# Landmark attention and MLP on one core: half the second layers by seven half-size products, W1 centred by GpSimd

## The chip, the cores and the metric

One Trainium2 chip, one core. The metric is the device time of one execution in microseconds (us), the median over several runs. A profiled execution, taken once, gives the trace from which the single durations come. Engines: PE (TensorE), DVE (VectorE), ACT (ScalarE), POOL (GpSimd), SP (SyncE, which here issues most transfers).

## The reference

q, k and v are (8 batches, 8 heads, 576 tokens, 64) in float32. Attention is approximated through 32 landmarks per head, each the mean of 18 neighbouring tokens; the MLP stands behind it with a residual.

```python
A  = sm(q, k_lm);  Bm = sm(q_lm, k_lm);  C = sm(q_lm, k)     # softmax(scale * a @ b^T)
Z  = Bm^T / (norm1(Bm) * norminf(Bm) + 1e-6)
for _ in range(6):
    Z = 2 * Z - Z @ Bm @ Z
x  = heads side by side of (A @ Z @ C @ v)                    # (8, 576, 512)
xn = (x - mean) / sqrt(var + 1e-6) * g_ln                     # over the 512 columns
out = x + relu(xn @ W1) @ W2                                  # W1 512 x 2048, W2 2048 x 512
```

## The kernel before

All matmul operands are float16, sums in PSUM and the stream x are float32. Every instruction goes through a small helper that keeps the program's order on its engine, so in the profile nearly all of DVE, ACT and POOL stand on line 69 and all matmuls on line 75; groups are told apart by tiles. The order of the work is therefore the order in which the Python code issues it.

**Attention.** Batches come as 0, 1, 2, then the pairs (3, 4) and (5, 6), then 7. `Coming` prepares the queries, keys and values of a batch or pair: SP loads into a staging buffer `stg`, POOL casts to float16 (`nat`, `natv`), DVE turns 32x32 blocks (`turn`, tile `xT`), landmark sums come from POOL (`asum`, `s`) or DVE (`part`), and a matmul spreads them (`spread`). `next_cast` and `next_job` each take one such piece; `prepare(c, casts, jobs)` takes several. `attention2` is a generator: scores against landmarks (tiles psb, psec, psea), the gram and its row and column sums, six iterations of Z on 32x32 tiles (tile `st`: DVE scales, PE multiplies, hand over hand), then `rows_of`, which writes x in 36 blocks of 128 tokens (`xblk`) through PE and ACT and takes their variance on DVE (`block_done`). The softmax quotient of A is a multiplication of `ea` by reciprocals (`normalize`, line 734): by POOL, in batch 1 by DVE.

**MLP.** LayerNorm is folded in. Its mean is taken out of W1: `less_mean(f)` computes the negative column mean of quarter f, and `center_w1` adds it to W1 (eight DVE instructions of 128x1024, in the first eight steps of batch 2's attention); batches 0 and 1 use W1 as it is with a correction. Its 1/deviation is multiplied in at the end (`rstds`, from ACT in `deviations`). The first layer never forms x: `product_of_heads(f)` multiplies the small Z side with a quarter of W1 (tile `m`), `chunk(m)` multiplies that by A, four matmuls of 288 columns, and ACT writes the relu into 128 of the 2,048 hidden columns (`hT`). The second layer takes, for each of the 4 or 5 row blocks of a batch, 16 matmuls of 128x512 into one PSUM bank; `finish_block` adds bank times rstd into x on DVE and `store` sends it out on SP's queue. Even batches have four blocks; the last 64 tokens go with the next odd batch (`keep_tail`, POOL), which has five.

**How they interleave.** `mlp()` is one stream of matmul columns: the second layer of batch b, and every 2,048 columns a piece of the first layer of batch b+1. `fill(n)` draws n x 512 columns from it between the steps of the attention generators; the list `steps` says how many, and how many casts and jobs of the next set are done in each. Behind the last attention the stream runs on by itself. Batch 0's first layer is written out by hand in the loop over m before that, with the first two row blocks of its second layer accumulated beside it and batch 1's scores behind its chunk 12.

PSUM: four single banks handed out by turns (`banks`; one of them goes to attention, so three remain; tile `bank` in the profile), and two tiles of two banks each (`ps2`: psh, psea, psec, psd, pscv, pszt, pszc).

Of the kernel before, what the change touches and what calls it, by code (L numbers as in the profile page):

```python
# [9 lines left out]
FP16 = mybir.dt.float16  # L10
# [3 lines left out]
ALU = mybir.AluOpType  # L14
AX = mybir.AxisListType

P = 128
# [3 lines left out]
def kernel(  # L21
# [13 lines left out]
    DM = H * D  # L35
# [5 lines left out]
    KCH = DM // P  # L41
    MCH = HID // P
# [11 lines left out]
        name=nc.get_next_instruction_name(), act_func_set_id=6, ins=[], outs=[]))  # L54
# [3 lines left out]
    stage = ctx.enter_context(tc.tile_pool(name="stage", bufs=6))  # L58
# [12 lines left out]
    dve, pool, scalar = Ordered(nc.vector), Ordered(nc.gpsimd), Ordered(nc.scalar)  # L71
    act = scalar.activation

    def MM(o, l, r, rb=0, cb=0, start=True, stop=True, skip=False):
        keep(nc.tensor.matmul(o, l, r, start=start, stop=stop, tile_position=(rb, cb),  # L75
                              skip_group_check=(skip or cb != 0)))
# [85 lines left out]
    for i in range(NV):  # L162
        t = const.tile([P, U, NJ, 2, D + 1], FP16, name=f"natv{i}")
# [18 lines left out]
    w1_16 = wpool.tile([P, KCH, HID], FP16, name="w1_16")  # L182
    w2_16 = wpool.tile([P, MCH, DM], FP16, name="w2_16")
# [6 lines left out]
    def less(f):  # L190
        return less_[f // 2][:, f % 2, :]
# [77 lines left out]
    banks = Banks()  # L269
# [6 lines left out]
    x_blk = {}  # L276
# [40 lines left out]
    def normalize(ea, engine):  # L317
        engine.tensor_tensor(out=ea, in0=ea, in1=divisors(ea), op=ALU.mult)
# [196 lines left out]
    class Coming:  # L515
# [25 lines left out]

        def next_job(self):
            if self.jobs:
                f, i = self.jobs.pop(0)
                f(i)

        def load(self, i, queue=nc.sync):
# [116 lines left out]
    def attention2(bs, c):  # L664
        units, lm, xT = c.units, c.lm, c.xT
        W = len(units)
# [21 lines left out]
        ea = []  # L688
# [31 lines left out]
        late, z0 = bs[0] == 1, 2 if bs[0] == 1 else 0  # L720
# [8 lines left out]
        for it in range(6):  # L729
            st = iterate(p1, st, it, W)  # L730
            if it < W // 2:
                ea += scores_q((2 * it, 2 * it + 1), lm, xT)
            if W // 2 <= it < W // 2 + W:
                normalize(ea[it - W // 2], dve if late else pool)
            if late and it == 4:
                product(0)
            if late and it == 5:
                product_done()
            yield it < W // 2
# [30 lines left out]
    stats_of, rstds = {}, {}  # L770
# [16 lines left out]
    def deviations(b):  # L787
        n = 4 + b % 2
        if b not in rstds and blocks_done.get(b) == n:
            lnv = mstat.tile([P, 5], FP32, name="lnv", tag="lnv")  # L790
            act(lnv[:, 0:n], stats_of[b][:, 0:n, 1], AF.Ln, bias=eps_ln[:], scale=UP * UP)
            rstds[b] = mstat.tile([P, 5], FP32, name="rstd", tag="rstd")
            act(rstds[b][:, 0:n], lnv[:, 0:n], AF.Exp, scale=-0.5)

    def store(j, x, cols, both=False):
        for i in range(2):
            b, c = divmod(2 * j + i, NJ)
            half = x[ds(64 * i, 64), cols]
# [17 lines left out]
        if c1 == KCH:  # L816
            scalar.copy(less(f), psf_of.pop(f)[:])

    def center_w1(f, c=0, n=KCH):
        o = w1_16[:, ds(c, n), ts(f, 512)]  # L820
        dve.tensor_tensor(out=o, in0=o, in1=less(f)[:, None, :].broadcast_to([P, n, 512]),
                          op=ALU.add)

    class First:
        def __init__(self, b):
# [12 lines left out]

        def product_of_heads(self, f):
            self.m16[f] = mprod.tile([P, U, 512], FP16, name="m16", tag="m16")  # L840
            psm = [banks.take([P, 512]) for _ in range(U)]
            for r in range(2):
                for e in range(2):
                    for u in range(U):
                        rows, cb = ds(64 * e, 64), 32 * (2 * (e ^ u) + r)
                        MM(psm[u][ds(cb, 32), :], self.zt[rows, r, self.w0 + u, :],
                           w1_16[rows, 2 * u + r, ts(f, 512)], rb=64 * e, cb=cb,
                           stop=self.sums is None, skip=True)
            for u in range(U):
                if self.sums is not None:  # L850
                    MM(psm[u], self.sums[:, u, :], less(f), start=False, skip=True)
                if u == 0 or f == 0:
                    scalar.copy(self.m16[f][:, u, :], psm[u])
                else:
                    dve.tensor_copy(out=self.m16[f][:, u, :], in_=psm[u])

        def chunk(self, m):
            psh = ps2.tile([P, 2, 512], FP32, name="psh", tag="p2")
# [21 lines left out]
    def keep_tail(b):  # L880
        if b % 2 == 0:
            room_for(b + 1)
            pool.tensor_copy(out=hTs[b + 1][:, :, 0:64], in_=hTs[b][:, :, S - 64:S])

    def finish_block(b, u, pso, part=None):
# [8 lines left out]
        if part != 0:  # L894
            x_blk.pop(j)

    def second_layer(b):
        hT = hTs[b]
        blocks = range(4 + b % 2) if b else (2, 3)
        for u in blocks:  # L900
            last = b == B - 1 and u == 4
            for part in ((0, 1) if last else (None,)):
                n = DM if part is None else DM // 2
                cols = ts(part or 0, n)
                pso, bank = banks.hold([P, n]), banks.last
                for m in range(MCH):
                    MM(pso[:], hT[:, m, ts(u, P)], w2_16[:, m, cols],
                       start=(m == 0), stop=(m == MCH - 1))
                    if m >= 8:
# [54 lines left out]
    sets = [Coming((1,), ("k0", "k1", "q0", "q1"))]  # L964
# [9 lines left out]
    def prepare(c, casts, jobs):  # L974
        for _ in range(casts):
            if c.casts and (c.parts[c.casts[0]][0] == "v" or len(c.n16) < 6):
                c.next_cast()
                load_ahead()
        for _ in range(jobs):
            c.next_job()  # L980

    warm(36, 160)
    a0 = attention0()
# [14 lines left out]
    b1 = sets[0]  # L998
# [31 lines left out]
    def blocks_0_and_1(m):  # L1030
        for u in range(2):
            MM(accs[u][:], hTs[0][:, m, ts(u, P)], w2_16[:, m, :],
               start=(m == 0), stop=(m == MCH - 1))

    a1 = attention2((1,), b1)
    for m in range(MCH):
        l1.chunk(m)
        if m == 0:
            scale_w1(7, 1, scalar)
        if m == 1:  # L1040
            l1.product_of_heads(1)
# [12 lines left out]
        if 2 <= m < 10 or m == 13:  # L1054
            b1.next_job()
        if m >= 10:
            blocks_0_and_1(2 * (m - 10))
            blocks_0_and_1(2 * (m - 10) + 1)
    keep_tail(0)
    for m in range(12, MCH):  # L1060
        blocks_0_and_1(m)
        if m == 12:
            assert not b1.jobs
            banks.order.remove(3)
            next(a1)
            deviations(0)
    for u in range(2):
        finish_block(0, u, accs[u])
# [7 lines left out]
    for c, after, plan in zip(sets, sets[1:] + [None], steps):  # L1076
        while c.jobs:
            prepare(c, 1, 1)
            fill(5)
        attention = a1 if c is b1 else attention2(c.bs, c)  # L1080
        for i, ((count, casts, jobs), quiet[0]) in enumerate(zip(plan, attention)):
# [37 lines left out]
```

## Time and profile before

| | |
|---|---|
| median of 3 runs | 319.45 us (319.11 to 320.27) |
| profiled execution | 318.92 us |
| its span, first to last instruction | 317.1 us |
| granted TensorE clock | 0.998 |
| PE busy | 280.5 us (88%) |
| ACT busy | 181.7 us (57%) |
| DVE busy | 169.5 us (53%) |
| POOL busy | 126.7 us (40%) |

Busy shares are means over a kernel with stages: the first 40 us wait for data, from 40 to 115 us attention of the first batches runs with little MLP work beside it, from 160 us on PE is nearly full, and from 296 us only the second layer of batch 7 is left. Timeline rows read: start, duration, engine, line, operation, output<-inputs, shapes, how many, and in brackets the idle time before with what released it. Group rows read: line, engine, operation, output<-inputs, shapes, how many | busy us, mean ns of one | idle before, releaser. Chain rows read: start, length, what the time went to.

### The profile page before, as it was taken

The page shows a single profiled execution, that of the slowest core. Times are in us where ns is not written, and L with a number is a line of the kernel's source. Part 1 is how long each engine was busy: PE and PEld are TensorE (multiplying, and loading weights), DVE is VectorE, ACT ScalarE, POOL GpSimd, SP SyncE. Part 2 cuts the span into 40 slices and gives each one's busy share as a digit, 9 for nine tenths or more (in the row PEclk, how much of TensorE's full clock was granted, in tenths as well). Part 3 has the DMA queues.
Part 4 walks back from the last instruction along what each step waited for, and adds up shares of the span by engine and source line. Part 5 has one row for each costly group of instructions (what it writes and reads, how often), then busy time and mean ns, then how long its engine had stood idle before and what let it go on. Part 6 is the DMA issues. An engine that isn't in the chain of part 4 may idle for free. (4 is left out here: it accounts for less than half of the span.)

```text
span 317.1 us, 8209 instructions
## 1 busy us (share of the span) xinstructions
PE 280.5 (88%) x3439; PEld 149.7 (47%) x3439; DVE 169.5 (53%) x378; ACT 181.7 (57%) x315; POOL 126.7 (40%) x155
## 2 busy tenths in 40 slices
PE   8868996887885797887999999989999999999995
PEld 7534652344432344444544544545554456355544
DVE  2654946667898664336994972555442344121112
ACT  3479865178640674876668549576649465444300
POOL 5387748742469974653927423210003000100000
PEclk9999999999999999999999999999999999999999
DMA  7999997459527949600895261111111112213133
GB/s 258 388 389 386 388 235 285 128 131 293 192 55 233 294 118 321 198 2 9 207 277 166 55 169 33 33 35 35 33 37 34 35 34 50 51 33 68 33 87 82
DMA packets 23486, 46.68 MB, mean 147 GB/s; under 512 B 2324, under 2 KB 2584, under 8 KB 23448
## 3 DMA queue, kind: packets, MB, share of 16 engines
q1 hardware_dynamic: 23288, 46.02, 48.4%
q8 instruction: 27, 0.44, 0.6%
q10 hardware_dynamic: 160, 0.13, 0.2%
q14 instruction: 11, 0.09, 0.1%
HBM read 36.70 MB, written 9.44 MB: 146 GB/s over the span
## 5 line engine op out<-in xcount | busy, mean ns | idle before, releaser
L75 PE MATMUL bank<-w,hT 128*128 128x512 f16 (+1 forms) x592 | 151.0, 374 | 0.7 <-DVE m L69 0.4
L69 ACT ACTIVATE hT<-psh 128x576 f16<-128x576 f32 x128 | 81.5, 650 | 46.4 <-PE psh L75 45.4
L75 PE MATMUL psh<-ea,m 128*128 128x288 f16 x512 | 82.8, 286 | 6.4 <-ACT m L69 2.6
L75 PEld LDWEIGHTS <-hT 128*128 128x128 f16 x592 | 54.7, 98 | 48.5 <-issue 9.5
L75 PEld LDWEIGHTS <-m 128*128 128x128 f16 x512 | 49.0, 97 | 39.0 <-ACT m L69 6.3
L69 DVE SCALAR_TENSOR_TENSOR xblk<-bank,rstd,xblk 128x512 f32<-128x512 f32 (+1 forms) x37 | 26.8, 726 | 32.8 <-PE bank L75 32.7
L69 POOL CAST nat<-stg 128x1152 f16<-128x1152 f32 x28 | 33.1, 1194 | 23.8 <-DMA stg<-in_k_dram 9.9
L69 ACT COPY xblk<-bank 128x512 f32<-128x512 f32 (+1 forms) x40 | 23.3, 584 | 24.7 <-PE bank L75 24.6
L69 DVE BATCH_NORM_STATS2 six<-xblk 128x6 f32<-128x512 f32 x36 | 24.7, 686 | 23.0 <-ACT xblk L69 22.9
L69 POOL TENSOR_TENSOR ea<-ea,lns 128x576 f16<-128x576 f16 x12 | 15.4, 1283 | 51.5 <-ACT lns L69 45.1
L69 ACT CAST m<-bank 128x512 f16<-128x512 f32 x40 | 22.6, 586 | 16.5 <-PE bank L75 15.8
L69 DVE CAST m<-bank 128x512 f16<-128x512 f32 x24 | 16.4, 683 | 23.4 <-PE bank L75 21.3
L69 POOL CAST natv<-stg 128x1152 f16<-128x1152 f32 x16 | 18.3, 1162 | 26.5 <-DMA stg<-in_v_dram 23.9
L69 DVE SCALAR_TENSOR_TENSOR st<-st,bank 128x128 f16<-128x128 f16 (+2 forms) x36 | 11.3, 313 | 28.6 <-PE bank L75 28.6
L69 DVE TENSOR_REDUCE part<-xT 128x32 f16<-128x576 f16 x32 | 22.4, 742 | 0.1
L69 DVE STREAM_TRANSPOSE xT<-nat 128x576 uint32<-128x576 uint32 x28 | 21.3, 760 | 0.4 <-POOL nat L69 0.4
L75 PE MATMUL bank<-w,zt 64*32 64x512 f16 x256 | 17.0, 386 | 3.5 <-ACT xblk L69 2.3
L75 PE MATMUL bank<-zcbd,ea 128*128 128x256 f16 (+1 forms) x80 | 15.6, 274 | 3.4 <-ACT m L69 1.7
L69 POOL COPY hT<-hT 128x1024 f16<-128x1024 f16 x4 | 4.1, 1037 | 34.6 <-PE bank L75 26.2
L69 POOL TENSOR_TENSOR asum<-asum 128x256 f32<-128x256 f32 (+1 forms) x24 | 15.4, 643 | 1.9
L75 PEld LDWEIGHTS <-st 32*32 32x32 f16 x448 | 5.7, 89 | 19.2 <-DVE st L69 9.0
L75 PE MATMUL bank<-st 32*32 32x64 f16 (+1 forms) x384 | 9.3, 189 | 6.0 <-DVE st L69 5.9
(113 smaller groups left out, 264.4 us busy)
## 6 DMA issues: line engine op xcount, KB each, us to landing
stg<-in_q_dram SPq DMA_DIRECT2D x16, 576.0 KB, 6.4
stg<-in_k_dram SPq DMA_DIRECT2D x16, 576.0 KB, 7.0
out_dram<-xblk SPq DMA_DIRECT2D x70, 128.0 KB, 2.4
wstg<-in_moe_w_ch_dram SPq DMA_DIRECT2D x16, 512.0 KB, 7.1
stg<-in_v_dram SPq DMA_DIRECT2D x9, 576.0 KB, 5.7
stg<-in_v_dram SPq DMA_DIRECT2D x14, 288.0 KB, 5.5
out_dram<-xblk ACTq DMA_DIRECT2D x2, 64.0 KB, 2.2
out_dram<-xblk SPq DMA_DIRECT2D x2, 64.0 KB, 1.9
```

The costliest lines, as they stand in the source:

```text
L69: return lambda *args, **kw: keep(getattr(self.engine, op)(*args, **kw))
L75: keep(nc.tensor.matmul(o, l, r, start=start, stop=stop, tile_position=(rb, cb), skip_group_check=(skip or cb != 0)))
```

## The change

**Second layer of batches 4 to 7.** Blocks 0 to 3 of a batch are seen as a 2 x 2 matrix product: h (512 tokens by 2,048) in quarters h11, h12, h21, h22 by token halves of 256 and hidden halves of 1,024, W2 likewise. Seven products of quarters with sums and differences (Winograd's form) replace eight. Each product is 2 row tiles x 8 matmuls of 128x256. Called P1 to P7 in their order here, with the banks they write: P1 h12·w21 (pe), P2 h11·w11 (pa), P3 s2·t2 on top of it (pa), P4 (h11-h21)·t3 on top (pa), P5 s1·t1 (pc), P6 (h12-s2)·w22 on top (pc), P7 h22·t4 (pd). A bank is not finished before it is used: `add` multiplies a running sum by rstd into one or two quarters of x, and the next product goes on in the same bank. Per batch DVE gets four sums for s1 and s2 and four differences in place, all of 128x1024 in float16, and 16 `add` instructions of 128x256 where there were four of 128x512. Block 4 of odd batches is done as before. The sums of W2's quarters, t1 to t4, are formed once by POOL, 16 instructions of 128x512, after the last cast, in the staging buffers.

**W1's centring** goes from DVE to POOL, 16 instructions of 128x512 in place of eight of 128x1024; one is issued with each call of `prepare` after batch 1's product of heads has read that quarter.

**Batch 1.** Its scores are issued behind chunk 14 of batch 0, and its gram ahead of the last four accumulations into blocks 0 and 1 and of their two updates on DVE; the first step of the plan goes. Its two normalising multiplications go from DVE to POOL. A `turn` is issued only when enough casts have been.

```diff
         def next_job(self):
             if self.jobs:
-                f, i = self.jobs.pop(0)
+                f, i = self.jobs[0]
+                n = len(self.units)
+                if f == self.turn and 3 * n - len(self.casts) < min(i + 3, 2 * n):
+                    return
+                self.jobs.pop(0)
                 f(i)
...
-                normalize(ea[it - W // 2], dve if late else pool)
+                normalize(ea[it - W // 2], pool)
...
-    def center_w1(f, c=0, n=KCH):
-        o = w1_16[:, ds(c, n), ts(f, 512)]
-        dve.tensor_tensor(out=o, in0=o, in1=less(f)[:, None, :].broadcast_to([P, n, 512]),
-                          op=ALU.add)
+    uncentered = []
+    def center_w1(f, c):
+        o = w1_16[:, c, ts(f, 512)]
+        pool.tensor_tensor(out=o, in0=o, in1=less(f), op=ALU.add)
...
         (product_of_heads)
+            if self.b == 1:
+                uncentered.extend((f, c) for c in range(KCH))
...
+    HK, HN = MCH // 2, DM // 2
+    FAST = 4
+    def mixes_of_w2():
+        w2_mix.extend(stage.tile([P, HK, HN], FP16, name=f"w2mix{i}", tag="stg") for i in range(6))
+        t1, t2, t3, t4 = w2_mix[:4]
+        for o, x, y, op in ((t3, w22, w12, ALU.subtract), (t2, t3, w11, ALU.add),
+                            (t4, w21, t2, ALU.subtract), (t1, w12, w11, ALU.subtract)):
+            for k in range(0, HK, 2):
+                pool.tensor_tensor(out=o[:, k:k + 2, :], in0=x[:, k:k + 2, :],
+                                   in1=y[:, k:k + 2, :], op=op)
+                yield
+    def seven_products(b):
...
+        def product(to, left, right, first=True):
+            for i in range(2):
+                for k in range(HK):
+                    MM(to[:, i, :], left[:, k, ts(i, P)], right[:, k, :],
+                       start=first and k == 0 and i == 0, stop=k == HK - 1, skip=True)
+                    yield HN
+        def add(half, col, t):
+            for i in range(2):
+                u = 2 * half + i
+                o = x[u][:, ts(col, HN)]
+                dve.scalar_tensor_tensor(out=o, in0=t[:, i, :], scalar=rstds[b][:, u:u + 1],
+                                         in1=o, op0=ALU.mult, op1=ALU.add)
+        for k in range(0, HK, 4):
+            n = ds(k, 4)
+            dve.tensor_tensor(out=s1[:, n, :], in0=h21[:, n, :], in1=h22[:, n, :], op=ALU.add)
+            dve.tensor_tensor(out=s2[:, n, :], in0=s1[:, n, :], in1=h11[:, n, :],
+                              op=ALU.subtract)
+        pe, ie = bank()
+        yield from product(pe, h12, w21)
...
+        add(0, 0, pe)
+        banks.release(ie)
+        mix(h21, h11, h21, ALU.subtract)
+        pa, ia = bank()
+        yield from product(pa, h11, w11)
+        add(0, 0, pa)
+        mix(h12, h12, s2, ALU.subtract)
+        yield from product(pa, s2, t2, False)
+        add(0, 1, pa)
+        yield from product(pa, h21, t3, False)
+        add(1, 1, pa)
+        add(1, 0, pa)
+        banks.release(ia)
+        pc, ic = bank()
+        yield from product(pc, s1, t1)
+        add(1, 1, pc)
+        yield from product(pc, h12, w22, False)
+        add(0, 1, pc)
+        banks.release(ic)
+        for u in range(2):
+            store(j0 + u, x[u], ts(0, DM))
+        pd, i_d = bank()
+        yield from product(pd, h22, t4)
+        add(1, 0, pd)
+        banks.release(i_d)
+        for u in range(2, 4):
+            store(j0 + u, x[u], ts(0, DM))
...
     def second_layer(b):
+        if b >= FAST:
+            for _ in mixes_left:
+                pass
+            yield from seven_products(b)
+            blocks = blocks[4:]
...
         (prepare)
+        if uncentered:
+            center_w1(*uncentered.pop(0))
...
         (loop over batch 0's chunks)
+        if m == 14:
+            assert not b1.jobs
+            banks.order.remove(3)
+            next(a1)
...
     keep_tail(0)
+    next(a1)
     for m in range(12, MCH):
         blocks_0_and_1(m)
-        if m == 12:
-            assert not b1.jobs
-            banks.order.remove(3)
-            next(a1)
-            deviations(0)
+    deviations(0)
...
-    steps = [[(4, 0, 0)] + 6 * [(3, 0, 0)] + [(4, 1, 0)] + 5 * [(6, 1, 1)]]
+    steps = [6 * [(3, 0, 0)] + [(4, 1, 0)] + 5 * [(6, 1, 1)]]
...
-            if c is sets[1] and i < 8:
-                center_w1(i // 2, 2 * (i % 2), 2)
             fill(count)
             if after:
                 prepare(after, casts, jobs)
+            if c is sets[3] and not sets[4].casts:
+                for _ in range(2):
+                    next(mixes_left, None)
```

More of the change, by code (lines that the diff above doesn't have):

```diff
@@ L840, in product_of_heads @@
             self.m16[f] = mprod.tile([P, U, 512], FP16, name="m16", tag="m16")
+            assert self.b < 2 or (f, KCH - 1) not in uncentered
             psm = [banks.take([P, 512]) for _ in range(U)]
@@ L895, in finish_block @@
             x_blk.pop(j)
+    HK, HN = MCH // 2, DM // 2
+    FAST = 4
+    w2_mix = []
+    mixes_left = []
+    def mixes_of_w2():
+        w11, w12 = w2_16[:, 0:HK, 0:HN], w2_16[:, 0:HK, HN:DM]
+        w21, w22 = w2_16[:, HK:MCH, 0:HN], w2_16[:, HK:MCH, HN:DM]
+        w2_mix.extend(stage.tile([P, HK, HN], FP16, name=f"w2mix{i}", tag="stg") for i in range(6))
[6 more added lines that the diff above has]
+                yield
@@ new lines, in seven_products, with mix, bank @@
+    def seven_products(b):
+        hT = hTs[b]
+        t1, t2, t3, t4, s1, s2 = [t[:] for t in w2_mix]
+        w11, w22 = w2_16[:, 0:HK, 0:HN], w2_16[:, HK:MCH, HN:DM]
+        w21 = w2_16[:, HK:MCH, 0:HN]
+        h11, h12 = hT[:, 0:HK, 0:256], hT[:, HK:MCH, 0:256]
+        h21, h22 = hT[:, 0:HK, 256:512], hT[:, HK:MCH, 256:512]
+        j0 = 9 * (b // 2) + 4 * (b % 2)
+        x = [x_blk.pop(j0 + u) for u in range(4)]
+        def mix(o, left, right, op):
+            for k in range(0, HK, 4):
+                dve.tensor_tensor(out=o[:, k:k + 4, :], in0=left[:, k:k + 4, :],
+                                  in1=right[:, k:k + 4, :], op=op)
+        def product(to, left, right, first=True):
[10 more added lines that the diff above has]
+                                         in1=o, op0=ALU.mult, op1=ALU.add)
+        def bank():
+            return banks.hold([P, 2, HN]), banks.last
+        for k in range(0, HK, 4):
+            n = ds(k, 4)
[4 more added lines that the diff above has]
+        yield from product(pe, h12, w21)
+        deviations(b)
+        while b not in rstds:
+            yield 0
+            deviations(b)
+        add(0, 0, pe)
[25 more added lines that the diff above has]
+            store(j0 + u, x[u], ts(0, DM))
+        if b % 2 == 0:
+            hTs.pop(b)
@@ L1053 @@
             next(a0)
-        if 2 <= m < 10 or m == 13:
+        if 2 <= m < 10:
             b1.next_job()
+        if m == 13:
+            b1.next_job()
+        if m == 14:
+            assert not b1.jobs
+            banks.order.remove(3)
+            next(a1)
         if m >= 10:
@@ L1080 @@
         attention = a1 if c is b1 else attention2(c.bs, c)
+        mixes_left = mixes_of_w2() if c is sets[3] else mixes_left
         for i, ((count, casts, jobs), quiet[0]) in enumerate(zip(plan, attention)):
-            if c is sets[1] and i < 8:
-                center_w1(i // 2, 2 * (i % 2), 2)
             fill(count)
```

## The prediction

> **What bounds the kernel now.** I read the page first, then the chain that ended last, then PE's timeline for its gaps, then the rows of the instructions that the change moves.
>
> ```profile
> PE 280.5 (88%) x3439; PEld 149.7 (47%) x3439; DVE 169.5 (53%) x378; ACT 181.7 (57%) x315; POOL 126.7 (40%) x155
> PE 39%; ACT 4%; issue 1%; DVE 1%; ACTq 0%
> ```
>
> PE is busy for 280.5 of 317.1 us. So time can come from two places: fewer matmul columns, or the 36.6 us in which PE waits. The change tries both. The end of the chain is pure streaming:
>
> ```profile
> 269.30 2.17 PE bank L75 x10
> 271.50 0.76 DVE xblk L69
> ...
> 295.09 0.98 PE psh L75 x8
> 296.07 17.32 PE bank L75 x96
> ```
>
> The last line is batch 7's second layer: 64 matmuls of 512 columns and 32 of 256, 40,960 columns at 0.423 ns each. One of 512 is thus 0.217 us (the first line, 2.17/10, agrees) and one of 256 is 0.108. The second line is the one place here where PE stood until DVE had emptied a bank: it paid the whole DVE instruction.
>
> The idle notes of PE's timeline (in brackets) show where the early stalls are:
>
> ```profile
> 50.10 0.23 PE L75 MATMUL bank<-st 32*32 32x64 f16 x6 [1.30 <-DVE st L69]
> 55.17 0.24 PE L75 MATMUL bank<-st 32*32 32x64 f16 x8 [1.39 <-DVE st L69]
> 56.80 0.24 PE L75 MATMUL bank<-st 32*32 32x64 f16 x8 [0.64 <-DVE st L69]
> ...
> 84.16 0.66 PE L75 MATMUL psh<-ea,m 128*128 128x288 f16 x4 [0.70 <-DVE cv L69]
> 93.33 0.24 PE L75 MATMUL bank<-st 32*32 32x64 f16 x8 [0.68 <-DVE st L69]
> 96.54 0.22 PE L75 MATMUL bank<-st 32*32 32x32 f16 x8 [1.57 <-DVE st L69]
> 99.45 0.24 PE L75 MATMUL pszt<-st,cv 32*64 32x32 f16 x8 [1.29 <-DVE st L69]
> 102.01 0.60 PE L75 MATMUL bank<-zcbd,ea 128*128 128x256 f16 x2 [0.77 <-DVE zcbd L69]
> ```
>
> All eight wait for a small DVE step that stands behind a long DVE instruction: the first three (3.3 us) behind block updates and batch 1's multiplies, the other five (5.0 us) behind the centring of W1 and turns.
>
> **Seven products: the saving.** Per batch, 112 matmuls of 256 columns (28,672) take the place of 64 of 512 (32,768): 4,096 x 0.423 ns = 1.73 us, and 6.9 us for four batches. Each half-size matmul needs its own weight load, 98 ns in the page's group, which 108 ns just covers. Weighed against a rule: the Trainium skill ("TensorE: Matmul & The Clock Gate", Back-to-back issue gap) gives load-and-matmul pairs 81 ns at 128 columns and 131 at 512, hence as an estimate 98 at 256. By it a batch would go from 8.4 to 11.0 us, a loss of 10.4 us in all, and it speaks against halving. The last stretch above shows both widths at one price per column, so the row decides.
>
> **Seven products: new waits.** P2, P3 and P4 write the same bank, and so do P5 and P6. Between them DVE must add the bank into the stream, and the first matmul of the next product waits for the second of the two adds. One such wait costs two adds of 128x256:
>
> ```profile
> 48.09 1.37 DVE L69 SCALAR_TENSOR_TENSOR xblk<-bank,rstd,xblk 128x512 f32<-128x512 f32 x2
> ...
> 313.41 0.48 DVE L69 SCALAR_TENSOR_TENSOR xblk<-bank,rstd,xblk 128x256 f32<-128x256 f32 x1 [1.26 <-PE bank L75]
> ```
>
> Two of 128x512 take 1.37 us where one takes 0.74, so about 0.1 overlaps, and two of 128x256 take 0.89. With about 0.06 of handoff a boundary is 0.95 us. What hides it would be a first-layer chunk (four matmuls of 288 columns, 0.49 us), issued every 2,048 columns. In the order of the changed program these fall in the middle of the products (4 matmuls, chunk, 8, chunk, 4): none stands at P2 to P3 or P3 to P4, one at P5 to P6. That leaves 0.95 + 0.95 + 0.46 = 2.36 us per batch, 9.4 for four; batch 7 has no chunks, +0.5. Sum 9.9, more than the 6.9 saved.
>
> Further waits: in batches 4 and 6 P2 takes a bank that ACT has just to empty (586 ns, the m row): +0.6 each, 1.2. In batch 4 DVE also carries the rows' statistics (686 + 182 ns per block) and the adds queue behind them: I take +1.5 over four boundaries, bounds 0 and 4. In batch 7 DVE's queue itself is the bound: two sums s1, s2, two adds, two differences, two adds before P3. The 128x1024 operations have only the row of 840 ns (0.65 to 0.69 where POOL is quiet), so 2 x 0.7 + 0.89 + 2 x 0.7 + 0.89 = 4.6 us after the last hidden chunk, against 0.65 (ACT) later start and 2.8 us of P1 rest and P2: P3 waits about 2.0 instead of 0.95. +1.0, bounds 0 and 2. The stores move from four blocks' ends to two points per batch, on SP's queue, which is idle there; the last of them still follows block 4. The 16 mixes of W2 cost nothing on the path: POOL's last value cast ends at 189 us, it is then nearly idle (2.3 us busy in 200 to 240), and 16 x 1.15 = 18.4 us end near 214, about when batch 4's P3 first reads t2. If that cover were gone, P3 would wait for one operation, 1.2 us.
>
> Second layers together: -6.9 + 9.9 + 1.2 + 1.5 + 1.0 = +6.7, I take +6.5. Below: boundaries at 0.75 (half an add hidden) and none of the further waits, about +1. Above: all upper bounds and 840 ns operations, about +11.
>
> **Early part.** What moves, and its rows:
>
> ```profile
> L69 DVE TENSOR_TENSOR w<-w,less 128x1024 f16<-128x1024 f16 x8 | 6.7, 840 | 0.0
> L69 DVE TENSOR_TENSOR ea<-ea,lns 128x576 f16<-128x576 f16 x2 | 3.0, 1514 | 1.4 <-ACT lns L69 1.4
> L69 POOL TENSOR_TENSOR ea<-ea,lns 128x576 f16<-128x576 f16 x12 | 15.4, 1283 | 51.5 <-ACT lns L69 45.1
> L69 POOL TENSOR_TENSOR asum<-nat 128x512 f32<-128x512 f16 x12 | 14.2, 1184 | 1.0
> ```
>
> DVE loses 6.7 + 3.0 = 9.7 us. POOL gains 16 pieces of 128x512. No row has that shape in f16: 512/576 of 1,283 gives 1.14, the f32 row gives 1.18; with 1.15 that is 18.4 us, and with two multiplies of 1.28, 21 us. The Trainium skill ("GPSIMD Engine Reference", Engine selection) advises VectorE for two-input elementwise work, GpSimd being about 2x slower. The centring rows agree (1.15 per 512 against 0.84 per 1,024), the multiplies do not (1,283 against 1,514); by the rule these would take 6.1 us of POOL instead of 2.6.
>
> With the gram ahead of two block updates (1.37 us) and the multiplies off DVE, I take 2.5 of the first 3.3 us. Up to 77 us, though, the turns and sums of batch 2's keys on DVE bind, so 1.5 arrives there. Of the 5.0 us behind centring, most could go. But POOL has to take 21 us where it had this idle time, and nothing after it:
>
> ```profile
> 64.56 1.16 POOL L69 CAST natv<-stg 128x1152 f16<-128x1152 f32 x1 [2.24 <-DMA stg<-in_v_dram]
> 76.21 1.15 POOL L69 CAST nat<-stg 128x1152 f16<-128x1152 f32 x1 [6.89 <-DMA stg<-in_k_dram]
> 89.46 1.28 POOL L69 TENSOR_TENSOR ea<-ea,lns 128x576 f16<-128x576 f16 x1 [6.38 <-PE bank L75]
> ```
>
> With two gaps of about 1 us that is 17.7 us of room for 21; from 89 to 115 it is full. The pieces, one per preparation step, push the casts and landmark sums of the next pair back by some 2 to 3 us, so of 1.5 + 5.0 I keep 4.5. Bounds: 6.5 (all stalls gone, POOL keeps up) and 1 (the next pair's sums come late). From 124 us POOL had slack (3.79 us idle), so what is won there is kept. The gate on turns only reorders DVE; the moved scores are the same instructions sooner. Both at nothing; a turn held back wrongly would cost its 0.76 us.
>
> **Sum.** 317.1 - 4.5 + 6.5 = 319.1 us of span, 1.8 around it as now, 320.9 against the profiled 318.9; the median of the runs is 0.5 higher: 321.5 us.
>
> **Rivals.** *Faster (0.30).* The early stalls go in full and part of the adds' boundaries is covered, because attention steps and row blocks happen to stand there in batches 4 and 5: -6 + 2.5 = -3.5, 316 us. It decides where the second layers lose less than the early part wins. For: PE's early gaps are plain queueing on DVE, and DVE loses 9.7 us. Against: in batches 6 and 7 no such work exists. *Much slower (0.25).* POOL's queue, 21 us into 17.7, becomes what batches 2 and 3 wait for, and the early part brings 1.5 only; with DVE's operations at 840 ns the second layers cost 8.5: +7, 326.5 us. It decides where a POOL sum of the next pair comes later than PE has other columns for. *The saving is not there*: if weight loads stretch the pitch from 108 to 115 ns, 448 matmuls give back 3.1 us, 324.5; inside the second rival's share.
>
> **Numbers.** Forecast 0.45, rivals 0.30 and 0.25. A measurement tells 0.5%, about 1.6 us, from no change. The forecast's own range is 318.5 to 325; its lower part and the upper part of the first rival give 0.17 within that bound; faster 0.30, slower 0.53. The range for 8 in 10 goes from the first rival's value to a little past the second's: 315.5 to 327.5.
>
> **What would show it.** After: PE's rows of batch 7's end 19 to 20 us where 17.32 stands; gaps of 0.9 to 1.0 released by DVE's xblk at P3 and P4 in each of four batches, near 0.5 at P6; the span up to about 200 us shorter by 4.5; PE busy down to about 273.5; the five gaps behind centring gone, POOL full from 76 to 124. I am wrong if batches 4 to 7 take no longer than now, or if the early part does not arrive sooner.

## The result, and the profile after

The changed kernel takes 344.52 us (median of 4 runs, 342.91 to 346.09), the kernel before 319.51: a ratio of 1.078, interval 1.072 to 1.084. The sign of the forecast was right and its size was not: 25.0 us slower where 2 were forecast, and outside the range. The profiled execution took 346.09 us, the longest of the four; its span is 344.4. Some kernels below also had single executions in a slower state, at a lower granted clock: the ratios leave these out, the medians do not.

The page after, busy line, the row of the granted clock in 40 slices of 8.6 us, and the chain by engine:

```profile
PE 289.5 (84%) x3631; PEld 173.8 (50%) x3631; DVE 202.1 (59%) x448; ACT 182.5 (53%) x315; POOL 160.5 (47%) x189
...
PEclk9967999999996987999999999868999999999999
...
PE 61%; ACT 14%; DVE 13%; issue 4%; DMA 4%; POOL 2%; SPq 0%; DVEq 0%; POOLq 0%; ACTq 0%
```

The clock row before:

```profile
PEclk9999999999999999999999999999999999999999
```

PE streams fewer columns and is busy 9 us longer. The clock row says why: before it held nines throughout, now there are four dips. The trace's clock record gives full or half clock and nothing between; until the last matmul 34 us of this execution are at half clock, from 20, 102, 126, 222 and 232 us on. The kernel before has none until its last matmul.

The dip at 222 us stands behind a long stall of PE. PE's idle notes, batch 4 to batch 7 (some of the larger ones):

```profile
225.14 0.59 PE L75 MATMUL bank<-zcbd,ea 128*128 128x256 f16 x2 [5.49 <-DVE m L69]
231.97 1.03 PE L75 MATMUL bank<-w2mix,w2mix 128*128 128x256 f16 x4 [2.27 <-DVE xblk L69]
237.77 0.60 PE L75 MATMUL bank<-w2mix,hT 128*128 128x256 f16 x4 [1.13 <-DVE xblk L69]
246.58 0.92 PE L75 MATMUL bank<-w,hT 128*128 128x256 f16 x7 [1.34 <-DVE xblk L69]
...
302.24 0.60 PE L75 MATMUL bank<-w2mix,w2mix 128*128 128x256 f16 x4 [0.97 <-DVE xblk L69]
306.09 0.60 PE L75 MATMUL bank<-w2mix,hT 128*128 128x256 f16 x4 [0.97 <-DVE xblk L69]
312.68 1.03 PE L75 MATMUL bank<-w,hT 128*128 128x256 f16 x8 [0.53 <-DVE xblk L69]
325.64 1.91 PE L75 MATMUL bank<-w2mix,w2mix 128*128 128x256 f16 x16 [1.32 <-DVE xblk L69]
```

The rows of 0.97, 0.97 and 0.53 us are batch 6's boundaries P2 to P3, P3 to P4 and P5 to P6, as forecast (0.95, 0.95 and 0.46) to 0.07 us. The 5.49 us were not. DVE's and POOL's timelines at that place:

```profile
215.64 5.94 DVE L69 TENSOR_TENSOR w2mix<-hT 128x1024 f16<-128x1024 f16 x1
221.67 0.69 DVE L69 TENSOR_TENSOR w2mix<-w2mix,hT 128x1024 f16<-128x1024 f16 x1
...
224.43 0.66 DVE L69 CAST m<-bank 128x512 f16<-128x512 f32 x1
```

```profile
215.57 2.26 POOL L69 TENSOR_TENSOR w2mix<-w 128x512 f16<-128x512 f16 x2
217.77 1.04 POOL L69 COPY hT<-hT 128x1024 f16<-128x1024 f16 x1
218.77 2.26 POOL L69 TENSOR_TENSOR w2mix<-w 128x512 f16<-128x512 f16 x2
```

The first of batch 4's four sums (half of s1) takes 5.94 us, the three behind it 0.69 each. It ends 0.55 us after POOL's last sum of W2, at 221.03: by that it stood until POOL was done and then ran. Two more runs with the same products and POOL's sums in the same order show it too, with 5.96 us (`chunk_at_boundary`) and 4.12 us (`late_only`), each ending 0.55 us after POOL's last instruction. Behind it in DVE's queue was the emptying of a bank (tile m, at 224.43) that PE needed. PE stood, and the windows behind run slowly for 15 us (window and length, then the busy time of PE, its weight loads, DVE, ACT and POOL, then the granted clock, the share of DMA and GB/s):

```profile
220.00:225.00 5.00, 0.00 (x0) 0.00 (x0) 4.84 (x7) 0.00 (x0) 1.03 (x1) 0.65 0.00 0
225.00:230.00 5.00, 4.56 (x25) 3.11 (x24) 2.85 (x7) 2.16 (x4) 0.00 (x0) 0.66 0.01 3
230.00:235.00 5.00, 3.03 (x14) 2.09 (x15) 2.84 (x6) 0.85 (x2) 0.00 (x0) 0.68 0.00 0
```

The following table serves all that follows. It gives the end of batch 3's last update of x (DVE's xblk rows), and for each later batch the time from the last update of the batch before it to its own, all in us, from the profiled executions.

| kernel | end of batch 3 | batch 4 | batch 5 | batch 6 | batch 7 |
|---|---|---|---|---|---|
| before | 208.8 | 29.6 | 33.8 | 23.6 | 18.0 |
| the change | 213.8 | 41.1 | 39.4 | 25.0 | 21.6 |
| early_only | 214.1 | 30.3 | 36.6 | 23.6 | 18.0 |
| late_only | 212.3 | 35.7 | 41.0 | 25.0 | 21.6 |
| before_six | 210.0 | 29.6 | 33.8 | 25.0 | 21.6 |
| before_alternating | 208.2 | 29.6 | 33.8 | 21.2 | 17.9 |
| alternating_multiplies | 206.7 | 29.6 | 33.8 | 21.2 | 17.9 |
| before_fewer_cols | 219.5 | 28.4 | 36.2 | 23.6 | 18.0 |

### The profile page after: what moved, and what is told of

Its sections match the earlier page's. It is cut to its first block, busy times and chain, and to the rows that moved or that the text cites. A ratio compares the mean times of both kernels' runs of the same rounds, so it can differ in the third digit from the quotient of the medians.

```text
span 344.4 us, 8711 instructions
## 1 busy us (share of the span) xinstructions
PE 289.5 (84%) x3631; PEld 173.8 (50%) x3631; DVE 202.1 (59%) x448; ACT 182.5 (53%) x315; POOL 160.5 (47%) x189
## 4 chain that ended last, share of the span: by engine, by line
PE 61%; ACT 14%; DVE 13%; issue 4%; DMA 4%; POOL 2%; SPq 0%; DVEq 0%; POOLq 0%; ACTq 0%
PE bank L75 41%; PE psh L75 15%; ACT hT L69 5%; DVE xblk L69 5%; DMA wstg<-in_moe_w_ch_dram 3%; ACT m L69 3%; ACT xblk L69 2%; DVE w2mix L69 2%; DVE six L69 2%; ACT lns L69 2%; PE psd L75 1%; DMA stg<-in_k_dram 1%; PE psec L75 1%; PE pscv L75 1%; PE psea L75 1%
## 5 line engine op out<-in xcount | busy, mean ns | idle before, releaser
L75 PE MATMUL bank<-w,hT 128*128 128x512 f16 (+1 forms) x528 | 114.9, 341 | 6.3 <-DVE xblk L69 3.6
L75 PE MATMUL psh<-ea,m 128*128 128x288 f16 x512 | 86.7, 296 | 9.2 <-ACT hT L69 4.5
L75 PEld LDWEIGHTS <-hT 128*128 128x128 f16 x656 | 62.1, 99 | 44.1 <-issue 19.9
L69 DVE SCALAR_TENSOR_TENSOR xblk<-bank,rstd,xblk 128x256 f32<-128x256 f32 (+1 forms) x85 | 42.3, 535 | 26.3 <-PE bank L75 22.0
L69 POOL TENSOR_TENSOR ea<-ea,lns 128x576 f16<-128x576 f16 x14 | 17.9, 1284 | 62.9 <-ACT lns L69 62.9
L69 ACT COPY xblk<-bank 128x512 f32<-128x512 f32 (+1 forms) x40 | 23.3, 583 | 27.8 <-PE bank L75 27.7
L75 PE MATMUL bank<-w,zt 64*32 64x512 f16 x256 | 18.8, 413 | 5.3 <-DVE xblk L69 2.4
L75 PE MATMUL bank<-w2mix,w2mix 128*128 128x256 f16 x128 | 18.4, 283 | 5.5 <-DVE xblk L69 5.5
L75 PE MATMUL bank<-w2mix,hT 128*128 128x256 f16 x128 | 16.9, 272 | 4.0 <-DVE xblk L69 4.0
L69 POOL TENSOR_TENSOR w<-w,less 128x512 f16<-128x512 f16 x16 | 18.4, 1158 | 2.6 <-PE bank L75 2.6
L75 PEld LDWEIGHTS <-w2mix 128*128 128x128 f16 x128 | 12.6, 101 | 8.5 <-issue 3.8
```

What stands on the lines that cost most here:

```text
L69: return lambda *args, **kw: keep(getattr(self.engine, op)(*args, **kw))
```

## The experiments

All ratios are against runs of the kernel before on the same chip; its medians there were 318.4 to 319.2 us. Kernels that did not stand on the same chip are best compared by these ratios.

**The two halves.** `early_only` has FAST = 8 and no sums of W2. `late_only` is the kernel before with only `seven_products`, `mixes_of_w2` and FAST = 4.

> The change without the seven products and without the sums of W2: only the early part (centring on POOL, batch 1's scores, gram and multiplies). Theory A (the early part is about neutral, since what it wins by 98 us, 3.5 us, is lost to a lower granted clock near 20, 100 and 125 us and to POOL's queue): 319 to 326 us, with the granted clock again below 0.99. Theory B (the early part is the gain that was forecast, and the dips of the clock do not belong to it): 314 to 316 us, clock 0.99 or more.

Measured: 325.03 us (322.87 to 327.54), ratio 1.019 (1.011 to 1.027).

> The kernel before with only the seven products of batches 4 to 7 and the sums of W2 on POOL. Theory A (nearly all of the loss is here: the sum s1 of batch 4 held up by POOL, the low clock behind it, and the boundaries of 0.97 us): 335 to 340 us. Theory B (the early part is a gain, so the late part costs still more than the whole change): 345 to 350 us. Theory C (the early part costs about as much as the late part): 330 to 333 us.

Measured: 338.88 us (336.32 to 340.91), ratio 1.059 (1.051 to 1.067). The late part costs 20.5 us, the early part 6.6; the sum, 27.1, is near the 25.0 of the whole. Both times lie in theory A's ranges; which of the causes that it names carries how much is asked next. The early part is no gain: the execution of `early_only` at a granted clock of 0.989 took 322.87 us, that of the kernel before at the same clock 319.63. So part of the 6.6 us goes with the clock.

**Batch 4's first sum.** In `from_batch5` batch 4 keeps its usual second layer; in `mixes_chained` POOL's sums come in an order in which half of them need the one directly before:

```diff
-    FAST = 4
+    FAST = 5
```

```diff
-        for o, x, y, op in ((t3, ...), (t2, ...), (t4, ...), (t1, ...)):
-            for k in range(0, HK, 2):
+        for k in range(0, HK, 2):
+            for o, x, y, op in ((t3, ...), (t2, ...), (t4, ...), (t1, ...)):
```

> The change with the seven products in batches 5, 6 and 7 only (FAST = 5); the sums of W2 stay where they are. Theory A (DVE's first sum of batch 4 waits for POOL's run of W2 sums, PE stands for 5.5 us and the granted clock falls to 0.65 for 15 us): 330 to 334 us, no PE wait over 2.5 us behind 200 us and clock 1.0 there. Rival (batch 4 costs only its boundaries, as the others): 340 to 343 us.

Measured: 336.53 us (334.31 to 339.12), ratio 1.055 (1.046 to 1.063). 8 us less than the whole change, a little short of theory A's 10 to 14; the edit also takes away batch 4's boundaries, so the 8 us are not the stall's alone. Two of theory A's signs fail: behind 200 us a half clock of 3.4 us is left, at 269, and ahead of it a PE wait of 2.71 us at batch 5's boundary P5 to P6. There DVE idles for 2.83 us, because the adds stand in its queue behind a row statistic whose block of x ACT has not written yet.

> The change with the 16 sums of W2 in another order on POOL: slice by slice t3, t2, t4, t1, so that t2 must wait for t3 and t4 for t2, and POOL's run is broken where before it was not. Theory A (DVE's two-input sum can enter at a break in POOL's run, and only there): the sum s1 of batch 4 takes 1 to 3.5 us instead of 5.94, PE's wait of 5.5 us falls below 3.5 and the clock behind it stays above 0.9: 336 to 341 us. Rival (DVE waits until POOL has nothing left, broken or not): the sum takes 5 us or more, 343 to 346 us.

Measured: 341.01 us (338.08 to 341.78), ratio 1.067 (1.059 to 1.075), at the upper end of theory A's range. DVE's timeline of this run:

```profile
215.83 0.87 DVE L69 TENSOR_TENSOR w2mix<-hT 128x1024 f16<-128x1024 f16 x1
216.79 1.47 DVE L69 TENSOR_TENSOR w2mix<-w2mix,hT 128x1024 f16<-128x1024 f16 x1
218.19 1.64 DVE L69 TENSOR_TENSOR w2mix<-hT 128x1024 f16<-128x1024 f16 x1
219.86 1.41 DVE L69 TENSOR_TENSOR w2mix<-w2mix,hT 128x1024 f16<-128x1024 f16 x1
```

The same POOL work lies beside it, and now DVE gets in between: its four sums and POOL's instructions alternate (POOL's 1.15 us become 1.5 to 1.6), PE's wait of 5.49 falls to 2.87, and batch 4's stretch from 41.1 to 36.6 us. The time falls by 3.5 us, with intervals that overlap, and theory A's clock is not there: a half clock of 3.4 us still follows, at 224 us. So the order of POOL's sums, not their amount, decides whether DVE is held up for 5.3 us.

That breaks in POOL's run let DVE in is not shown. Three of the four sums got in where POOL's next instruction followed without idle time. So did the centring in the kernel before, which began beside the POOL multiplication of 89.46 us:

```profile
90.01 1.28 DVE L69 TENSOR_TENSOR w<-w,less 128x1024 f16<-128x1024 f16 x1
```

```profile
90.69 1.61 POOL L69 CAST nat<-stg 128x1152 f16<-128x1152 f32 x1
```

The multiplication ends at 90.74, DVE's addition 0.55 us later, and the cast that was next takes 1.61 us where others take 1.15. The Trainium skill ("SBUF — State Buffer", SBUF: two separate sides) says that an instruction of VectorE with two SBUF inputs and one of GpSimd exclude each other and that the one that starts first keeps the port pair for its whole instruction. The mutual exclusion is what the rows show, and in the kernel before DVE waited for the rest of one POOL instruction. In the change, however, it was kept out through five, not one; what sets that place apart is open.

**The boundaries.** `before_six` is `late_only` with FAST = 6. `before_alternating` has the same products and additions there in another order, with the fourth bank, which attention no longer uses, given back; the two differences formed in place change order too. In short:

```diff
-  P1(pe) P2(pa) P3(pa) P4(pa) P5(pc) P6(pc) P7(pd)
+  P1(pe) P2(pa) P5(pc) P3(pa) P6(pc) P4(pa) P7(pd)
+  banks.order.append(3)      # once, when batch 6 begins
```

> The kernel before with the seven products in batches 6 and 7 only, in the order of the change, and the sums of W2 on POOL; nothing of the early part. Theory A (waits of 0.97 us at the boundaries that PE cannot fill; batch 6 costs 1.4 us more and batch 7 3.6 more, as in the trace of the change): 323 to 325 us. Rival (what the trace shows in batches 6 and 7 comes from batch 4's delay before them): 318 to 320 us.

Measured: 325.31 us (324.76 to 326.48), ratio 1.021 (1.017 to 1.025). Theory A: batches 6 and 7 cost 6.6 us of themselves, 5.0 of it in their two stretches, which are those of the whole change to 0.1 us.

> As the run beside it with batches 6 and 7, but the products in another order, P1 P2 P5 P3 P6 P4 P7, so that two banks alternate and DVE empties one while PE fills the other; the bank that attention used is put back for it. The same products, sums and additions. Theory A (the boundaries are the cost, and the smaller number of columns is a gain once they are covered): no PE wait of 0.97 us behind 295 us, 4 to 6 us less than beside it, 318 to 320 us, about the kernel before or a little faster. Rival (half-size matmuls themselves cost the time: pitch and weight loads): less than 2 us below the run beside it.

Measured: 316.42 us (median), ratio 0.992 (0.989 to 0.996): 8.9 us below the run beside it and 2.3 below the kernel before. The last PE rows of its chain:

```profile
293.15 1.19 PE psh L75 x8
294.35 15.89 PE bank L75 x144
```

The 112 half-size matmuls of batch 7 and the 32 of its block 4 run without one break, in 15.89 us where 17.32 stood. The start-to-start pitch of the products is 0.1105 us. So half-size matmuls are a gain once the boundaries are covered. Theory A holds, with more than the 4 to 6 us expected and a time below its range. The new order and the fourth bank were not tried apart. The two stretches account for 7.5 of the 8.9 us (25.0 to 21.2 and 21.6 to 17.9); in the run beside it PE's waits in them were 0.75, 0.96, 0.97, 0.53, 1.32, 0.97 and 0.97, together 6.5. The last 1.4 us are not resolved.

In `chunk_at_boundary` a chunk is asked for at the last matmul of P2, P3 and P5:

```diff
-                if ahead and not done and owed >= gap and not quiet[0]:
+                if ahead and not done and (owed >= gap or want[0]) and not quiet[0]:
```

> The whole change, but a first-layer chunk (0.49 us of PE) is issued at each of the boundaries P2 to P3, P3 to P4 and P5 to P6 where one is still to come, instead of in the middle of a product. Theory A (the boundary is a wait of 0.95 us for two adds, of which PE's own work hides as much as stands there): the waits in batches 5 and 6 fall from 0.97 to 0.5 us, 341 to 343.5 us against 344.5. Rival (the chunk's own bank wait or ACT takes its place): no change within 1 us.

Measured: 343.28 us (341.44 to 344.46), ratio 1.074 (1.067 to 1.080). The time lies in theory A's range, at its upper end, but not for theory A's reason: batches 5 and 6 take 41.2 and 26.4 us where the change has 39.4 and 25.0. In each of the two falls a half clock of 3.4 us, by estimate a price of 1.7; without it they would be about as long as in the change. PE's and DVE's timelines in batch 6 show more:

```profile
300.47 1.47 PE L75 MATMUL bank<-w2mix,w2mix 128*128 128x256 f16 x12 [0.48 <-DVE xblk L69]
...
302.80 0.41 PE L75 MATMUL bank<-w,zt 64*32 64x512 f16 x8
304.84 1.03 PE L75 MATMUL bank<-w2mix,hT 128*128 128x256 f16 x8 [1.63 <-DVE xblk L69]
```

```profile
303.31 0.69 DVE L69 CAST m<-bank 128x512 f16<-128x512 f32 x1 [1.69 <-PE bank L75]
303.92 0.87 DVE L69 SCALAR_TENSOR_TENSOR xblk<-bank,rstd,xblk 128x256 f32<-128x256 f32 x2
```

At P2 to P3 the chunk hides its 0.49 us, as theory A says. At P3 to P4 the wait grows from 0.97 to 1.63: the first-layer piece that came up there was a product of heads (0.41 us of PE), and DVE empties its bank (m, 0.69) ahead of the adds. So what stands at a boundary must not need DVE itself.

**The early part.** `early_dve_centre` puts W1's centring back on DVE; `early_gram_only` also puts back the multiplies and takes out the gate on turns.

> The early part alone with W1's centring put back on DVE, in eight instructions as before; batch 1's scores and gram sooner and its multiplies on POOL stay, and so does the gate on turns. No seven products. Theory A (the 16 pieces on POOL push the casts and sums of batches 3 and 4 back by 5 us, and that is what made the early part slower): 316 to 320 us, the last landmark sum of that pair near 108 us again, no half clock near 100 us. Rival (the earlier gram or the multiplies on POOL are the cause): 323 to 326 us.

Measured: 323.6 us (322.43 to 326.83), ratio 1.016 (1.011 to 1.021). Centring is not the cause: theory A falls.

> Only batch 1's scores and gram sooner; centring and multiplies on DVE as before, no gate on turns, no seven products. Theory A: 317 to 319.5 us, a gain of 0 to 2 us of the 2.5 that was forecast for the rows of batch 1. Rival (the order of batch 1 is what costs): over 322 us.

Measured: 324.64 us (324.4 to 327.35), ratio 1.020 (1.016 to 1.025). The rival holds: the order of batch 1 alone costs as much as the whole early part. In `early_only` and `early_dve_centre` the stretches of batches 4 to 7 agree to 0.1 us (batch 5: 36.6 in both), so what is lost there does not come from the centring on POOL. My next theory was that the removed step's 2,048 columns are missed:

```diff
-    steps = [6 * [(3, 0, 0)] + ...
+    steps = [[(7, 0, 0)] + 5 * [(3, 0, 0)] + ...
```

> The early part alone (no seven products), with one number changed: the first step of the plan draws 7 x 512 columns of MLP work instead of 3 x 512, so that the 4 x 512 columns of the removed step are drawn after all. Theory A (the early part is slower because from there on the MLP stream lags 2,048 columns behind the attention, so that the attention of batch 7 stands with less beside it in batch 5's stretch, 36.6 us where 33.8 stood): batch 5's stretch back to 34 us, 320 to 322 us. Rival (POOL's load and the lower clock near 100 and 125 us are the cause): 324 to 326 us, as without this edit.

Measured: 325.14 us (324.17 to 329.11), ratio 1.019 (1.014 to 1.024). A miss for theory A: nothing gained, batch 5's stretch is 37.5, and the time lies in the rival's range.

> The same edit, with W1's centring on DVE as before (eight instructions); no seven products. Theory A: 317 to 319.5 us, about the kernel before or a little faster, batch 5's stretch at 34 us. Rival: 322 to 325 us, as the run with centring on DVE and without the edit.

Measured: 327.96 us (327.08 to 331.33), ratio 1.029 (1.023 to 1.035). A miss for both theories, and 4 us worse than without the edit (`early_dve_centre`). One number in the plan moves the time by 4 us, so the next runs asked for the plan alone, in the kernel before:

```diff
-    steps = [[(4, 0, 0)] + 6 * [(3, 0, 0)] + ...
+    steps = [[(0, 0, 0)] + 6 * [(3, 0, 0)] + ...
```

> The kernel before with one number changed: the first step of the plan draws no columns instead of 4 x 512. Every instruction is the same; the MLP stream only stands 2,048 columns later against the attention from there on. Theory S (the interleaving, not the moved work, is what costs behind 129 us): 321 to 325 us, and batch 5's stretch (from the end of batch 4's last block) longer than 33.8 us. Rival (order matters little, POOL's queue and DVE's are the cause): 318 to 320 us.

Measured: 328.3 us (326.04 to 330.76), ratio 1.030 (1.025 to 1.036): 9 us slower with the same instructions. The profiled execution, 11.9 us longer than the one before, has 4.2 us of it from a half clock at 18 us, ahead of the edit. Of the rest 1.7 lie in batch 0, 4.2 in batches 1 and 2, and 1.8 in batches 3 to 5 together (batch 5's stretch is 36.2). The execution at the highest clock, 0.992, took 326.04 us; the kernel before took 319.34 at 0.989. So some 7 us remain when the clock is alike.

> The kernel before with only the gate on turns. A held-back turn means one more round of preparation with its 5 x 512 columns, so the attention of each set stands 6 or so matmuls later in the MLP stream. Theory S: 320 to 324 us. Rival: 318 to 320 us.

Measured: 330.63 us (328.31 to 334.76), ratio 1.036 (1.031 to 1.040): the gate on turns alone costs 11 us, and 9 at like clock (328.31 us at 0.990). Before the last attention's scores 338 second-layer matmuls are issued instead of 330; in `before_fewer_cols` it is 328, in `early_gram_only` 328, in `early_only` 336. Both times lie above theory S's ranges: the direction is as it says, the size is not. The kernel is slower whichever way the stream moves, and the costs do not add up: `early_only` has both the gate and batch 1's new order and loses 6.6 us.

**What the moved work is worth without the shift.** On `before_alternating`, first with batch 1's multiplies on POOL, then with the centring too:

```diff
-                normalize(ea[it - W // 2], dve if late else pool)
+                normalize(ea[it - W // 2], pool)
```

> The faster kernel found so far (seven products in batches 6 and 7 in the alternating order, on the kernel before) with batch 1's two multiplies on POOL; no order, gate or plan changed. If the moved work itself is a gain without the shift: 314 to 316 us, the stalls of 1.39 and 0.64 us near 55 us gone. If POOL's queue takes it back: 316 to 318 us.

Measured: 314.35 us (314.18 to 316.98), ratio 0.9885 (0.985 to 0.992). The fastest kernel found, 1.2% (3.7 us) below the kernel before. The stalls near 55 us, 1.39 and 0.64 before and 0.71 and 0.64 without the edit, are gone, and batch 3 ends 1.5 us sooner than without it. Against `before_alternating` the intervals of the two ratios overlap; the spans of the profiled executions are 313.9 and 312.5.

> As the run beside it, and W1's centring on POOL in 16 pieces too. If the forecast's step on DVE's relief was right and the shift hid it: 312 to 315 us, the stalls of 0.7 to 1.6 us between 93 and 102 us gone. If POOL's queue delays the pair of batches 3 and 4: 316 to 320 us.

Measured: 316.98 us (median), ratio 0.991 (0.988 to 0.995). The centring's move brings nothing; the spans of the two profiled executions are equal (312.5 us). PE's idle notes of this run near 95 us:

```profile
94.94 0.24 PE L75 MATMUL bank<-st 32*32 32x32 f16 x8 [2.75 <-DVE st L69]
98.50 0.24 PE L75 MATMUL pszt<-st,cv 32*64 32x32 f16 x8 [0.65 <-DVE st L69]
```

The stalls of 0.68, 1.57, 1.29 and 0.77 us (4.3) became two of 3.4 together. The small steps now stand behind turns that wait for POOL, the first for a landmark sum (s), the second for a cast, and in POOL's queue the pieces of W1 stand between these.

`alternating_early` combines the early part (with the 4 x 512 columns drawn) and the alternating order from batch 6:

> A candidate for a faster kernel: the early part as changed, with the 4 x 512 columns drawn, and the seven products in batches 6 and 7 only, in the alternating order. If both reasons hold (covered boundaries gain 2.4 us against the kernel before; the early part is neutral or a gain of up to 3 us once the columns are drawn): 313 to 317 us. If POOL's centring costs in itself: 319 to 322 us.

Measured: 323.25 us (322.3 to 324.91), ratio 1.014 (1.009 to 1.019). That is above both ranges: the early part costs about 7 us here as well (2.2% between this ratio and that of `before_alternating`).

## Why the prediction was wrong

In the profiled executions the change is 27.3 us longer. 8.7 of it are there in `early_only` already, where -4.5 was forecast; batches 4 and 5 add 13.6 and batches 6 and 7 add 5.0, where the forecast's terms give about 3.4 each. So two parts failed: the early one, and batches 4 and 5.

- **"The 16 mixes of W2 cost nothing on the path": wrong.** I looked at whether POOL would be done in time for its readers (it was: t2 well before P3), not at what DVE does in the meantime. The cover asked for was PE's; the collision was with DVE's sums. Batches 4 and 5, between which part of batch 7's attention moved, took 80.5 us where `early_only` took 66.9: 13.6 more. With POOL's sums in the other order (`mixes_chained`, 36.6 and 39.4) 9.1 are left, most of them waits of batch 4 behind DVE's longer queue (PE's 2.87 us for m, then 1.88, 1.13 and 1.34 at its boundaries). The kernel before had a hint: the centring row's mean of 840 ns against 0.65 where POOL is quiet. I read it as a slower instruction with bounds 0.65 to 0.84 and not as a wait for POOL. Those waits lasted at most the rest of one POOL instruction, though, so a hold of 5.3 us could not be read from them.
- **A clock taken as given.** The sum had no term for it. Of the 34 us at half clock 27.8 are matmuls, by PE's rows, so that 13.9 us of PE's busy time are its price in that execution (280.5 + 13.9 less 4 x 1.43 saved is 288.7; 289.5 is on the page). What of it lies on the path differs: the early dips fall in part into times that wait for data anyway (batch 0 ends 2.0 us later than before, although 9.1 us of its matmuls are at half clock). The Trainium skill ("TensorE: Matmul & The Clock Gate", What's actually happening) describes a clock that is halved after an idle window of some 3.4 us; the stretches here last 3.4, 6.8 and 10.2 us and agree, but several of the windows ahead of them were not idle (see below). The stall of 5.49 us was paid again in this way: behind it eight matmuls of 128x256 took 1.86 us, ahead of it 1.04.
- **The gate and the moved scores "both at nothing": wrong.** Batch 1's new order alone costs 5.9 us (`early_gram_only`) and the gate alone 11, more than the whole early gain that I had forecast. Both shift attention against the MLP stream, and `before_fewer_cols` shows that such a shift alone costs 9 us with the same instructions. That the shift is all that the early part costs is argued, not shown: drawing the removed columns again did not bring the time back (325.14 us). My own sign came true, that the early part does not arrive sooner: batch 3 ends at 213.8 us instead of 208.8.
- **The early gain of 4.5: about a third was there.** Without the shift the multiplies bring some 1.4 us by the profiled spans, 2.1 by the medians; I had 1.5 for the gram and the multiplies together. The centring brings nothing where I counted on 3: my second rival, POOL's queue, is right in its mechanism. Two rows I had misread. Of the five stalls that I put behind the centring, those of 1.57 and 1.29 us stood behind turns that had themselves waited for POOL (0.96 us for a landmark sum, 0.37 for a cast). And the multiplies' 1,514 ns on DVE held a wait for POOL as well: in `before_six` the same two took 759 and 758.
- **Boundaries of 0.95: right** in size (0.97, 0.97, 0.53 in batch 6), in number, and in the verdict that they cost more than the columns save. With P2's start and batch 7's queue the forecast had 6.8 us of waits in batches 6 and 7 (2.36 + 0.6 + 2.85 + 1.0); 6.5 were there.
- **Saving of 1.73 us per batch: nearly right.** 112 x 0.1105 = 12.38 us against 64 x 0.2158 = 13.81: 1.43. The row decided rightly against the estimate of 98 ns and the rule's 131, by which the alternating order would have lost.
- **Batch 7: +3.6 where 2.1 stood.** Its three waits are 1.32, 0.97 and 0.97, less than forecast; but its last first-layer chunks now stand alone behind batch 6's products, 1.3 us from the end of batch 6's last update to P1 where 0.2 stood.

Open: why just this plan of columns is so much better than its neighbours was not traced stage by stage; why DVE was kept out through five POOL instructions in the change and through one elsewhere; and how the 9.1 us that are left in batches 4 and 5 divide. Open too is which windows end in a half clock: in the traces PE is busy for 60% or less in most that do, but windows of 54% in the kernel before did not. The half clock near 20 us comes in some executions and not in others of kernels that are the same up to there, the early ones of this study among them, so part of each difference of the early kernels is chance; the lowest times of `early_only`, `early_dve_centre` and `early_gram_only` (322.9, 322.4 and 324.4 us against 317.7) still show the loss.

## What to carry to other kernels

When work moves to an idle engine, ask not only whether it will be done in time, but what other engines have to do beside it: here DVE's additions and POOL's kept each other out, and another order of the same POOL work was worth 4.5 us of one batch. Where products go on in a bank that another engine must read first, try an order in which two banks alternate: here it turned a loss of 6.6 us from smaller matmuls into a gain of 2.3. A change that is worth 2 us must be measured without moving the interleaving of two streams, since moving that alone was worth 9 to 11 us here.

## What the runs showed of the hardware that I had not expected

A DVE addition of two SBUF tensors (0.69 us alone) took 5.94 us beside five POOL instructions, and 0.87 to 1.64 us each when the same POOL work came in another order; in the kernel before none of its kind took more than 1.28. The granted clock of TensorE went to one half for 3.4, 6.8 or 10.2 us after stretches of little PE work; within one of them eight matmuls of 128x256 took 1.86 us where eight took 1.04 before it. And at dense runs of small matmuls (pscv) PE stood for 1.45 us before and 2.59 after with "issue" as the only note; in the trace a 16 KB instruction transfer starts just there, at 124.6 us, in a stretch where the DMA share is 1.0; whether it is the cause was not tried.
